# A filter's hand-over between two steps: 16 block transpositions in SBUF in place of a round trip through DRAM

## The chip, the cores, the metric

The kernel runs on one core of a Trainium2 chip. The metric is the device time of one execution, in microseconds (us), as the median of several runs. All timed runs quoted here are of the fast state (the state in which executions of one kernel agree within some tenths of a per cent: ten of the kernel before took 2589.09 to 2597.96 us). A time that comes from a profile is the span of the profiled execution, which is some 2 us shorter than the timed figure of that same execution.

## The reference

A spectral filter along the sequence, then an MLP mixer; eight batches of 3008 x 256 floats.

```python
X = np.fft.rfft(x, axis=1)                        # x: (8, 3008, 256)
y = np.fft.irfft(X * (filt_r + 1j * filt_i)[None], n=3008, axis=1)
h = np.maximum(y.transpose(0, 2, 1) @ w_tok1, 0.0) @ w_tok2     # token mixing
u = y + h.transpose(0, 2, 1)
out = u + np.maximum(u @ w_ch1, 0.0) @ w_ch2                    # channel mixing
```

## The kernel before

The length 3008 is split as 64 x 47. The filter's *first step* (`a_unit`) is a product over the 64, with 12 tiles per batch. Its result has on each partition one pair of a frequency k2 (32 of them) and one of four parts, and along the row 24 places times 256 columns. The *second step* (`b_unit`, then `bi_unit`) takes, for one k2 at a time, the four parts times 24 places as 96 rows. So rows must change partitions in between. The kernel did this through a DRAM buffer `z`:

```python
def a_unit(b, c):
    ps = bank(free_bank())
    nc.tensor.matmul(ps, wa, xs.pop((b, c)).rearrange("p a d -> p (a d)"), start=True, stop=True)
    t1 = t1p.tile([P, XC, D], FP32, tag="t1", name="t1")          # two buffers
    nc.scalar.copy(out=t1.rearrange("p a d -> p (a d)"), in_=ps)
    nc.scalar.dma_start(rows_of(z_d, b)[:, ts(c, XC), :], t1)     # 256 KB out
# ... (cut) in dft(), second step:
    def t2_load(c):
        where, tag = (sp, "s") if first and c % 3 == 2 else (t2p, "t2")
        t2s[c] = where.tile([KR, KC, nb, D], FP32, tag=tag, name="t2")
        for i, b in enumerate(bs):
            nc.sync.dma_start(t2s[c][:, :, i, :], z_d[b, ts(c, KC)].rearrange("k r d -> r k d"))  # 192 KB in
    def b_unit(k):
        # ... (cut)
        nc.tensor.matmul(ps, wbs[k // WC][0:KR, k % WC, 0:P], t2s[k // KC][:, k % KC], start=True, stop=True)
        # ... (cut) fr, fi: the filter
        nc.vector.tensor_tensor(out=p1, in0=ps, in1=fr, op=ALU.mult)
        nc.vector.scalar_tensor_tensor(out=p2[re], in0=ps[im], scalar=-1.0, in1=fi, op0=ALU.mult, op1=ALU.mult)
        nc.vector.tensor_tensor(out=p2[im], in0=ps[re], in1=fi, op=ALU.mult)
```

The filters of batches 1 to 7 run beside the mixer of earlier batches. The first batch's filter has nothing to hide behind: it runs alone, beside the rounding of the mixer's 64-bit weights, and the mixer starts after it.

## Time and profile before

| | kernel before |
|---|---|
| time, median of 4 runs (beside the changed kernel) | 2592.37 us (2590.78 to 2594.97) |
| span of the profile | 2590.2 us |
| last matmul of the first step begins | 35.38 us |
| first product of the second step begins ("the mark") | 48.57 us |
| second step (first product to end of last product) | 76.99 us, to 125.56 |
| first matmul of the mixer begins | 169.77 us |

One more view: the DMA queues of the first 36 us. The columns are packets, MB, and share of the time of the 16 DMA engines; q1 is SyncE's queue, q10 ScalarE's, q0 GpSimd's.

```profile
q1 hardware_dynamic: 2930, 5.56, 56.2%
q10 hardware_dynamic: 1930, 2.93, 23.3%
q0 software_dynamic: 640, 0.58, 7.0%
```

Nearly all of the 23.3% are the stores of z (11 of 256 KB in this stretch).

### The profile page before, as it was taken

To read this page: it belongs to the slowest core of one execution; us is meant where nothing else is said; L and a number is where in the kernel's file an instruction comes from. 1 tells how busy PE (TensorE), PEld (TensorE's weight loads), DVE (VectorE), ACT (ScalarE), POOL (GpSimd) and SP (SyncE) were. 2 spreads that over 40 slices of the span, in tenths; PEclk is the share of its full clock that TensorE was granted. 3 is DMA by queue.
4 is the path that set the end of the run, shared out by engine and by line. 5 is a ranking of instruction groups with operands and counts; after the bars stand their busy time and mean duration, and the time that the engine had idled before them with its cause. 6 is when DMAs were issued, how large, how long until landed. Compare 5 with 4: busy or idle time off the path is not lost.

```text
span 2590.2 us, 31521 instructions
## 1 busy us (share of the span) xinstructions
PE 2510.2 (97%) x10952; PEld 2002.7 (77%) x10952; DVE 1795.7 (69%) x3441; ACT 691.2 (27%) x1347; POOL 527.7 (20%) x966
## 2 busy tenths in 40 slices
PE   6889999999999999999999999999999999999998
PEld 2556766788888777888887777788888888888887
DVE  3796888556575888745666788846678576647676
ACT  2433222123321222212231222212222122212222
POOL 3553111111211112112112111121121121211212
PEclk7999999999999999999999999999999999999999
DMA  8974333312332322203232223211232121100001
GB/s 235 251 199 154 110 100 110 109 48 85 95 90 63 88 82 77 80 13 93 90 95 79 75 83 86 81 32 57 90 85 74 51 64 52 25 9 8 17 12 21
DMA packets 156746, 211.43 MB, mean 82 GB/s; under 512 B 34648, under 2 KB 105410, under 8 KB 156588
## 3 DMA queue, kind: packets, MB, share of 16 engines
q1 hardware_dynamic: 84396, 118.80, 16.0%
q0 software_dynamic: 30656, 39.93, 6.4%
q10 hardware_dynamic: 41536, 50.69, 6.1%
q8 instruction: 87, 1.43, 0.2%
q14 instruction: 71, 0.58, 0.1%
HBM read 134.31 MB, written 74.97 MB: 81 GB/s over the span
## 4 chain that ended last, share of the span: by engine, by line
PE 76%; DVE 12%; ACT 2%; issue 2%; DMA 1%; ACTq 0%; DVEq 0%; POOL 0%; SPq 0%; POOLq 0%
PE ps_po L612 27%; PE ps_pg L578 16%; PE ps_pg L594 11%; PE ps_b L538 4%; PE ps_b L521 3%; DVE t L556 3%; DVE hh L556 2%; PE ps_acc L521 2%; PE ps_acc L538 2%; PE ps_b L543 2%; PE ps_acc L407 2%; DVE u L556 2%; PE ps_acc L475 1%; PE ps_b L475 1%; DVE s L556 1%
## 5 line engine op out<-in xcount | busy, mean ns | idle before, releaser
L556 DVE TENSOR_TENSOR hh<-ps_pg,s 128x512 f32<-128x512 f32 (+3 forms) x864 | 481.9, 585 | 626.4 <-ACT s L581 625.9
L657 POOL DMA_DIRECT2D out_dram<-r x757 | 410.6, 551 | 1948.7 <-ACT hh L599 928.4
L599 ACT ACTIVATE hh<-hh 128x512 f32<-128x512 f32 (+1 forms) x576 | 347.8, 621 | 1119.7 <-DVE hh L556 1119.7
L612 PE MATMUL ps_po<-t,wc 128*128 128x256 f32 (+1 forms) x2304 | 535.3, 375 | 5.1 <-DVE t L556 4.4
L612 PEld LDWEIGHTS ps_po<-t,wc 128*128 128x128 f32 x2304 | 434.6, 190 | 132.3 <-issue 54.1
L612 PE MATMUL ps_po<-hh,wc 128*128 128x256 f32 (+1 forms) x1728 | 413.2, 375 | 3.1 <-POOL wc L329 2.8
L578 PE MATMUL ps_pg<-v,wc 128*128 128x256 f32 (+1 forms) x1728 | 413.7, 375 | 0.8 <-POOL wc L328 0.7
L612 PEld LDWEIGHTS ps_po<-hh,wc 128*128 128x128 f32 x1728 | 327.5, 190 | 42.4 <-POOL wc L329 3.6
L578 PEld LDWEIGHTS ps_pg<-v,wc 128*128 128x128 f32 x1728 | 327.3, 190 | 41.4 <-DVE v L556 3.0
L594 PE MATMUL ps_pg<-u,wc 128*128 128x256 f32 (+1 forms) x1152 | 293.6, 377 | 7.4 <-DVE hh L556 7.0
L556 DVE TENSOR_TENSOR t<-t,hh 128x256 f32<-128x256 f32 (+1 forms) x576 | 242.0, 420 | 19.8
L594 PEld LDWEIGHTS ps_pg<-u,wc 128*128 128x128 f32 x1152 | 215.6, 190 | 43.8 <-DVE hh L556 17.7
L556 DVE TENSOR_TENSOR s<-ps_pg,hh 128x512 f32<-128x512 f32 (+1 forms) x288 | 196.1, 681 | 30.7 <-DVE hh L556 0.9
L556 DVE TENSOR_TENSOR t<-hh 128x512 f32<-128x512 f32 (+1 forms) x288 | 192.2, 667 | 0.6 <-ACT hh L599 0.6
L578 PE MATMUL ps_pg<-u,wc 128*128 128x256 f32 (+1 forms) x576 | 170.4, 378 | 3.0 <-DVE hh L556 3.0
L594 PE MATMUL ps_pg<-v,wc 128*128 128x256 f32 (+1 forms) x576 | 168.8, 375 | 0.0
L581 ACT COPY s<-ps_pg 128x256 f32<-128x256 f32 (+1 forms) x288 | 106.0, 368 | 153.2 <-PE ps_pg L578 150.1
L578 PEld LDWEIGHTS ps_pg<-u,wc 128*128 128x128 f32 x576 | 102.8, 191 | 22.1 <-issue 8.2
L594 PEld LDWEIGHTS ps_pg<-v,wc 128*128 128x128 f32 x576 | 108.5, 190 | 13.2
L521 PE MATMUL ps_b<-t,w 128*128 128x256 f32 x480 | 106.3, 384 | 3.2 <-ACT both L235 2.4
L538 PE MATMUL ps_b<-w,h 128*128 128x512 f32 (+1 forms) x232 | 107.7, 587 | 0.0
L475 PE MATMUL ps_acc<-p,wb 128*96 128x256 f32 (+1 forms) x256 | 95.4, 474 | 11.9 <-ACT t L481 7.3
(92 smaller groups left out, 2236.1 us busy)
## 6 DMA issues: line engine op xcount, KB each, us to landing
z_tmp<-t ACTq DMA_DIRECT2D x96, 256.0 KB
t<-z_tmp SPq DMA_DIRECT2D x128, 192.0 KB
g_tmp<-t ACTq DMA_DIRECT2D x128, 192.0 KB
x<-in_x_dram SPq DMA_DIRECT2D x184, 128.0 KB
out_dram<-r POOLq DMA_DIRECT2D x698, 32.0 KB, 1.8
t<-g_tmp SPq DMA_DIRECT2D x42, 512.0 KB
wb<-wbi_t SPq DMA_DIRECT2D x80, 224.0 KB
filt<-in_filt_r_dram SPq DMA_DIRECT2D x128, 48.0 KB
```

What stands on the lines that cost most here:

```text
L407: nc.tensor.matmul(ps, wa, xs.pop((b, c)).rearrange("p a d -> p (a d)"), start=True, stop=True)
L475: nc.tensor.matmul(ps[0:KR], wbs[k // WC][:, k % WC, P:], p, start=(i == 0), stop=(i == len(parts) - 1))
L521: nc.tensor.matmul(acc[:, t, :], w1[:, a, ts(t, P)], t4[b, a // TC4][:, a % TC4, :], start=(a == 0 and t == 0), stop=(a == A - 1 and t == ...
L538: nc.tensor.matmul(ps[:, 0:w], h1[:, t, ts(dh, P)], w2[:, t, ds(m * 512, w)], start=(t == 0), stop=False)
L543: nc.tensor.matmul(ps[:, ds(q * P, n)], t4[b, c][:, r, ts(dh, P)], wai[:, 0:n], start=False, stop=(q == 3))
L556: nc.vector.tensor_tensor(out=out, in0=in0, in1=in1, op=op)
L578: nc.tensor.matmul(ps[:, 0:hw], wc1[:, jp, n, :], mov, start=True, stop=True)
L581: nc.scalar.copy(out=s[:, 0], in_=g[0][:, 0, 0:hw])
L594: nc.tensor.matmul(ps[:, 0:hw], wc1[:, jp, n, :], mov, start=True, stop=True)
L599: nc.scalar.activation(out=hs, in_=hs, func=AF.Relu)
L612: nc.tensor.matmul(po[i][:, j, 0:hw], wc2[:, jp, n, :], mov, start=(jp == 0 and first == 1), stop=(jp == JP - 1 and last == 1))
L657: q.dma_start(rows[g, e, :, ds(h * A + 4 * m, n)], blocks[ts(g, CW), h, e, 0:n])
```

## The change

For batch 0 alone, `z` is replaced by a tile `turned` that holds all 24 places (and 8 of zeros, to make 32) by 256 columns. The first step's table is reordered, so that one part's 32 frequencies lie on 32 neighbouring partitions. Then 16 in-place transpositions of 32x32 blocks exchange frequency and place inside each group of 32 partitions. The second step's matmuls read 128 rows (with zero weights for the padding) straight from `turned`. The mixer's channel weights later take the tile's memory.

```diff
+    wa0 = wa.reshape(P, K2, 4).transpose(0, 2, 1).reshape(P, P)
+    wbi0 = wbi.copy()
+    wbi0[:, :, 0:P] = 0
+    wbi0.reshape(4, K2, K2, P + KR)[:, 0:A, :, 0:P] = wb.reshape(4, A, K2, P)
 ... (cut)
+    turned = wcp.tile([P, K2 * D + P], FP32, tag="wc", name="turned")
+    wa0 = turned[:, K2 * D:]
+    turned = turned[:, 0:K2 * D].rearrange("p (s d) -> p s d", d=D)
 ... (cut) a_unit:
-        nc.tensor.matmul(ps, wa, xs.pop((b, c)).rearrange("p a d -> p (a d)"), start=True, stop=True)
+        nc.tensor.matmul(ps, wa0 if b == 0 else wa, xs.pop((b, c)).rearrange("p a d -> p (a d)"), start=True, stop=True)
+        if b == 0:
+            nc.scalar.copy(out=turned[:, ts(c, XC), :].rearrange("p a d -> p (a d)"), in_=ps)
+            return
 ... (cut) between the steps:
+        if first:
+            for d in range(0, D, 16):
+                v = turned.rearrange("p s d -> p d s")[:, d:d + 16, :]
+                nc.vector.transpose(v, v)
 ... (cut) b_unit:
-            nc.tensor.matmul(ps, wbs[k // WC][0:KR, k % WC, 0:P], t2s[k // KC][:, k % KC],
-                             start=True, stop=True)
+            t2 = turned[:, k, :].unsqueeze(1) if first else t2s[k // KC][:, k % KC]
+            nc.tensor.matmul(ps, wbs[k // WC][0:P if first else KR, k % WC, 0:P], t2, start=True, stop=True)
 ... (cut) at the start:
+        nc.vector.memset(turned[:, A:K2, :], 0.0)
```

More of the change, by code (lines that the diff above doesn't have):

```diff
@@ L115, in _make_tables @@
     wbi[:, :, P:] = wi
-    return wa.astype(f), wai.astype(f), wbi.astype(f)
+    wa0 = wa.reshape(P, K2, 4).transpose(0, 2, 1).reshape(P, P)
+    wbi0 = wbi.copy()
+    wbi0[:, :, 0:P] = 0
+    wbi0.reshape(4, K2, K2, P + KR)[:, 0:A, :, 0:P] = wb.reshape(4, A, K2, P)
+    return wa.astype(f), wa0.astype(f), wai.astype(f), wbi.astype(f), wbi0.astype(f)
 @with_exitstack
@@ L132 @@
     nc = tc.nc
-    wa_np, wai_np, wbi_np = _make_tables()
+    wa_np, wa0_np, wai_np, wbi_np, wbi0_np = _make_tables()
     wa_d = nc.inline_tensor(wa_np, name="wa_t").ap()
@@ L139 @@
     wbi_d = nc.inline_tensor(wbi_np, name="wbi_t").ap()
+    wa0_d = nc.inline_tensor(wa0_np, name="wa0_t").ap()
+    wbi0_d = nc.inline_tensor(wbi0_np, name="wbi0_t").ap()
     z_d = nc.dram_tensor("z_tmp", (B, K2, KR, D), FP32, kind="Internal").ap()
@@ L148 @@
     glob = pool("glob", 1)
+    wcp = pool("wcp", 1)
     xp = pool("xp", XB)
@@ L188 @@
     w2 = glob.tile([P, TC, A * P], FP32, name="w2")
-    wc1 = glob.tile([P, JP, 7, P], FP32, name="wc1")
-    wc2 = glob.tile([P, JP, 7, P], FP32, name="wc2")
+    turned = wcp.tile([P, K2 * D + P], FP32, tag="wc", name="turned")
+    wa0 = turned[:, K2 * D:]
+    turned = turned[:, 0:K2 * D].rearrange("p (s d) -> p s d", d=D)
+    chan = []
     def raw(src, row, ap):
@@ L338, in wc1_load @@
         yield from rounded(st, 512, [(lambda v: v.rearrange("p (i j n) -> p i j n", j=2, n=P),
-                           wc1[:, 2 * q:2 * q + 2, slice(0, 5, 4) if c == 0 else slice(1, 7, 5)])], late)
+                           chan[0][:, 2 * q:2 * q + 2, slice(0, 5, 4) if c == 0 else slice(1, 7, 5)])], late)
         if c == DH - 1:
             for jp in range(2 * q, 2 * q + 2):
-                combine(wc1[:, jp:jp + 1])
+                combine(chan[0][:, jp:jp + 1])
     def wc2_load(i):
@@ L351, in tile_of @@
             return lambda v: v.rearrange("p (j g e i) -> p e j g i", j=2, e=DH, i=CW)[:, dh]
-        yield from rounded(st, 512, [(tile_of(dh), wc2[:, i, n].rearrange("p j (g i) -> p j g i", i=CW))
+        yield from rounded(st, 512, [(tile_of(dh), chan[1][:, i, n].rearrange("p j (g i) -> p j g i", i=CW))
                           for dh, n in ((0, slice(0, 2)), (1, slice(4, 7, 2)))], True)
-        combine(wc2[:, i:i + 1])
+        combine(chan[1][:, i:i + 1])
     LAST = ((wc2_load, 0), (wc1_load, 1), (wc1_load, 4), (wc2_load, 1), (wc1_load, 2), (wc2_load, 2), (wc1_load, 5),
@@ L421, in w_load @@
                 wbs[g] = wbp.tile([P, WC, P + KR], FP32, tag="wb", name="wb")
-                nc.sync.dma_start(wbs[g], wbi_d[:, ts(g, WC), :])
+                nc.sync.dma_start(wbs[g], (wbi0_d if first else wbi_d)[:, ts(g, WC), :])
             filt_load(c, first)
@@ L437, in dft @@
         t2s, t3s, prods = {}, {}, {}
+        if first:
+            for d in range(0, D, 16):
+                v = turned.rearrange("p s d -> p d s")[:, d:d + 16, :]
+                nc.vector.transpose(v, v)
         def t2_load(c):
-            where, tag = (sp, "s") if first and c % 3 == 2 else (t2p, "t2")
-            t2s[c] = where.tile([KR, KC, nb, D], FP32, tag=tag, name="t2")
+            if first:
+                return
+            t2s[c] = t2p.tile([KR, KC, nb, D], FP32, tag="t2", name="t2")
             for i, b in enumerate(bs):
@@ L577, in up_first @@
                            (g[1][:, 0], 6, vt[:, 0, 0:hw]), (g[1][:, 1], 4, vt[:, 1, 0:hw])):
-            nc.tensor.matmul(ps[:, 0:hw], wc1[:, jp, n, :], mov, start=True, stop=True)
+            nc.tensor.matmul(ps[:, 0:hw], chan[0][:, jp, n, :], mov, start=True, stop=True)
         s = sp.tile([P, 3, 256], FP32, tag="s", name="s")[:, :, 0:hw]
@@ L593, in up_last @@
                            (g[1][:, 1], 3, vt[:, 3, 0:hw])):
-            nc.tensor.matmul(ps[:, 0:hw], wc1[:, jp, n, :], mov, start=True, stop=True)
+            nc.tensor.matmul(ps[:, 0:hw], chan[0][:, jp, n, :], mov, start=True, stop=True)
         h = hh[:, :, 0:hw]
@@ L611, in down @@
         for i, j, first, last, n, mov in todo[part]:
-            nc.tensor.matmul(po[i][:, j, 0:hw], wc2[:, jp, n, :], mov, start=(jp == 0 and first == 1),
+            nc.tensor.matmul(po[i][:, j, 0:hw], chan[1][:, jp, n, :], mov, start=(jp == 0 and first == 1),
                              stop=(jp == JP - 1 and last == 1))
@@ L748 @@
     with tc.manual_schedule():
-        nc.sync.dma_start(wa, wa_d)
+        nc.sync.dma_start(wa0, wa0_d)
+        nc.vector.memset(turned[:, A:K2, :], 0.0)
         for t in filts:
@@ L755 @@
             if i == 0:
-                for t, src in ((wai_t, wait_d), (wai, wai_d), (ident, ident_d)):
+                for t, src in ((wai_t, wait_d), (wa, wa_d), (wai, wai_d), (ident, ident_d)):
                     nc.scalar.dma_start(t, src)
@@ L782 @@
         sum_up()
+        both = wcp.tile([P, 2, JP, 7, P], FP32, tag="wc", name="wc")
+        chan.extend((both[:, 0], both[:, 1]))
         for i in range(rounds, A // 2 + TC * N2 // NG):
```

## The prediction

> **What bounds the kernel now.** I read the page first, then the busy time by stretch, then the engines' timelines of the first 130 us, then the waits. The page says that the span as a whole belongs to TensorE:
>
> ```profile
> PE 2510.2 (97%) x10952; PEld 2002.7 (77%) x10952; DVE 1795.7 (69%) x3441; ACT 691.2 (27%) x1347; POOL 527.7 (20%) x966
> ```
>
> The change touches the filter of the first batch only, so what counts is when that filter runs and what bounds the kernel there. The busy time by stretch (length, then each engine's busy us with its instruction count, the granted clock, the DMA share, GB/s) shows it; I chose the cuts from the timelines (last matmul of the first step near 36, first product of the second step at 48.57, last one at 127, first matmul of the mixer at 169.77):
>
> ```profile
> 0.00:36.00 36.00, 18.95 (x23) 5.86 (x24) 9.45 (x15) 9.49 (x15) 11.07 (x24) 0.78 0.87 252
> 36.00:48.57 12.57, 6.12 (x9) 2.48 (x8) 0.00 (x0) 2.35 (x4) 0.00 (x0) 0.64 0.86 235
> 48.57:127.00 78.43, 70.04 (x236) 41.25 (x236) 64.98 (x144) 33.43 (x69) 47.71 (x87) 0.94 0.94 243
> ...
> 215.00:2590.00 2375.00, 2343.30 (x10412) 1903.03 (x10412) 1642.02 (x3134) 614.26 (x1203) 416.06 (x769) 1.00 0.24 69
> ```
>
> From 215 us on TensorE is busy 2343.3 of 2375 us; nothing of the change lies there, except that it begins earlier or later. Before 36 us no engine is full, but the DMA engines are (0.87, 252 GB/s). Between 36 and 48.57 VectorE does nothing at all, which is the time in which z goes to DRAM and comes back. From 48.57 to 127 VectorE has 65.0 of 78.4 us, and DMA is at 0.94. The VectorE and TensorE timelines show the hand-over (start, length, engine, line, operation, and in brackets the idle time before it with what ended it):
>
> ```profile
> 35.38 2.05 PE L407 MATMUL ps_acc<-x,wa 128*128 128x512 f32 x2 [5.71 <-DMA x<-in_x_dram]
> ...
> 47.29 1.19 PE L450 MATMUL ps_b<-t,wb 96*128 96x256 f32 x2 [6.45 <-DMA t<-z_tmp]
> ...
> 48.57 0.42 DVE L463 TENSOR_TENSOR p<-ps_b,filt 128x256 f32<-128x256 f32 x1 [13.26 <-PE ps_b L450]
> ```
>
> The last matmul of the first step waits for its input x, whose loads share the DMA engines with the stores of z. After it come copy, store, load, and the first matmul of the second step at 47.29. So 48.57 us is the mark: from there VectorE runs nearly without a break, and a shift of that mark shifts the mixer, and the end, by as much.
>
> [...] the output's block transpositions of 512 elements take 701 ns, hardly more than the 681 to 693 ns of a two-input operation of that size. [...] The new transpositions step by one whole row of 256 floats, 1 KB, on the read side and on the write side[...]. The kernel before has one such write, the sums into w at L263, which step by 512 bytes:
>
> ```profile
> L644 DVE STREAM_TRANSPOSE r<-u 128x512 f32<-128x512 f32 x80 | 56.1, 701 | 0.0
> ...
> L263 DVE TENSOR_TENSOR w<-both 128x384 f32<-128x384 f32 x8 | 6.6, 830 | 0.3
> L263 DVE TENSOR_TENSOR w<-both 128x192 f32<-128x192 f32 x2 | 1.0, 487 | 0.1
> ```
>
> 830 less 487 over 192 elements is 1.79 ns per element. Dense, 681 less 426 ns over 256 elements gives 1.0. [...] the trace has no strided read. [...] x waits while z is stored from another engine's queue (DMA share 0.87).
>
> **The change, part by part.**
> Removed: 12 stores of z of 256 KB from ScalarE's queue, 16 loads of 192 KB from SyncE's, hence 3 MB out and 3 MB in, and the round trip ahead of 47.29. ScalarE also loses five waits, 8.6 us together, for the two buffers that the stores emptied.
>
> First step. Up to 36 us, the DMA queues' table of that stretch gives 56.2% of the engines' time to SyncE's queue (x, weights, tables), 23.3% to ScalarE's (nearly all z: 2.75 of 2.93 MB), 7.0% to GpSimd's; 86.5% together. Without z's 21.9 points, the same work takes 35.4 x (1 - 21.9/86.5) = 26.4 us. TensorE sets a floor: twelve pairs of matmuls of 1.9 to 2.05 us at its reduced clock (0.78 here), from 4.8 us on, are 28 us. I take the last pair to begin at 27.5 rather than 35.4; with 2.05 for the pair, 0.6 for the copy and the signals, the transpositions begin at 30.
>
> Added: 16 transpositions of 128x512 on VectorE, in place, all of which must end before the first matmul of the second step (each of them has only 16 of the 256 columns of a row). Dense they would be 16 x 0.70 = 11.2 us. With the strided slope, 0.17 fixed + 512 x 1.79 ns = 1.08 us each, 17.3 in all. That covers the write; the read is strided too. If reading and writing overlap fully it stays near 1.1; if they add up, 1.5. I choose 1.15 us, and 0.03 between two: 16 x 1.18 = 18.9 us. VectorE is idle at that time, but the path goes through it: 30 + 18.9 + 1.3 (from matmul to first product, as 47.29 to 48.57) = 50.2 us. That is 1.6 later than 48.57. Hence at this mark the gain of the shorter first step is about eaten by the transpositions.
>
> Also added: a memset of 8 x 256 zeros ahead of the filters' (two times 0.91 us, in idle time; the filter loads start 2 us later, with slack). The matmuls of the second step read 128 rows instead of 96: same columns, same duration.
>
> Second step, 48.57 to 127. VectorE's work is unchanged: 65.0 us busy, some 69 with the gaps of 0.03 us. The other 9 to 10 us are waits, most of them after 100 us, for filter loads and what hangs on them (3.7 us directly for the imaginary part, 2.2 for ScalarE's copy of the real part, which itself waits 10.5 us for its load; some more for TensorE behind that). A filter load takes 5.2 us to land (median), 2.0 at best. Of 12787 packets in the stretch, 13 loads of z of 192 KB in 1 KB rows are some 2500, a fifth. With a fifth less, DMA is no longer at its limit and I expect about half of these waits to go: -5 us. From 127 to 170 VectorE is full (37.2 of 42.8 us) and ScalarE waits 4.5 us for weights; -1 us from a quieter DMA.
>
> Moved: the mixer's weights take the place of the turned tile, which is free long before they are written (last use near 127, first write at 164): no cost. The sum is +1.6 - 5 - 1 = -4.4 us: 2593.4 - 4.4 = **2589 us**.
>
> **Rivals.** (1) *VectorE takes the place of the round trip*: if each strided transposition costs 1.5 us or more, the mark goes to 56 or beyond, and eats the rest: 2594; at 2.3 us (read and write each twice as slow and one after the other) the mark lies at 69, +20 - 6 = 2607. For it: both sides are strided, the read is unmeasured. [...] (2) *The transpositions run at the dense 0.70 us*: the mark at 42.8, with -6: 2582; if the second step also loses nearly all its waits, 2578. For it: the dense rows; against it: L263. (3) *The DMA relief is hidden*: the first step is held by TensorE's clock and by the order of loads (its x and weights still take 56.2% of DMA time), so that it ends at 33; the waits in the second step are GpSimd's issuing (47.7 us busy in 78, six filter loads of 0.55 us per pair of units), and stay. Then +6 - 1: 2599. (4) *The gain or loss does not reach the end*, because a later stage absorbs it: between 127 and 170 VectorE and TensorE are 87% and 93% busy, and beyond 215 TensorE 98.7%, so I see nothing to absorb more than 2 us.
>
> **Range and chances.** The duration of the transpositions weighs most: 0.70 to 1.5 us are 13 us of mark, the first step's end adds 4 either way, the second step's waits 4. That gives 2576 to 2602, 8 in 10. Two per cent are 52 us, four fifths of the first 65 us of the kernel: neither a gain nor a loss of that size fits in a part that ends at 48.57. Faster by over 2%: 0.01; within: 0.97; slower: 0.02.
>
> **What would show it right or wrong.** In the profile after: a group of 16 transpositions with its mean (right if 1.0 to 1.3 us); the last matmul of the first step beginning at 26 to 30 us; the first product of the second step near 50; the DMA share of the second step clearly under 0.94, the filter waits about halved, its length near 73 us instead of 78.4; the first matmul of the mixer near 165; from 215 us the same busy times as before. The prediction is wrong if the transpositions have another duration, if each waits for a signal, if the copies into one shared tile make matmuls and copies of the first step take turns, or if the second step keeps its length with less DMA, because GpSimd's issuing set it.

The costs come from the trace of the kernel before: 701 ns for a dense transposition of 512 elements, and 1.79 ns per element with a step of 512 bytes on the write side against 1.0 dense. That 1.15 us lies near full overlap of reading and writing (1.1) and not near their sum (1.5) was the estimate. That the second step's matmuls take as long on 128 rows as on 96 was measured only afterwards (379 against 381 ns).

## The result and the profile after

Ratios here are the mean time of one kernel's fast runs over that of the other's fast runs of the same rounds, so they are not quite the ratio of the medians beside them.

| | before | after |
|---|---|---|
| time, median of 4 runs | 2592.37 us | 2589.48 us (2588.01 to 2591.14) |
| ratio | | 0.9988, 95% interval 0.9971 to 1.0005 |
| last matmul of the first step | 35.38 | 28.44 |
| the mark | 48.57 | 49.52 |
| second step | 76.99 us | 72.61 us |
| end of the last product to the mixer's first matmul | 44.21 us | 45.25 us |
| the mixer's first matmul | 169.77 | 167.38 |
| from there to the end | 2420.4 us | 2419.8 us |

The time is the same within 2%. The outputs are right. The profile's 3.0 us are the sum of the table's lines: +0.95 at the mark, -4.38 in the second step, +1.04 up to the mixer, -0.6 after it.

The timelines of TensorE and VectorE after the change, the same hand-over as in the prediction (start, length, engine, line, operation; in brackets the idle time and what ended it):

```profile
28.44 2.04 PE L417 MATMUL ps_acc<-x,turned 128*128 128x512 f32 x2 [2.57 <-DMA x<-in_x_dram]
...
48.24 1.19 PE L470 MATMUL ps_b<-turned,wb 128*128 128x256 f32 x2 [15.34 <-issue]
...
31.14 17.00 DVE L455 STREAM_TRANSPOSE turned<-turned 128x512 f32<-128x512 f32 x16 [1.87 <-ACT turned L419]
49.52 0.42 DVE L482 TENSOR_TENSOR p<-ps_b,filt 128x256 f32<-128x256 f32 x1 [1.39 <-issue]
```

TensorE's 15.34 us of idle time bear the label "issue" because the profile shows no releaser, but the transpositions end at 48.14 and the matmul follows at 48.24. A group's row gives the mean of the new operation:

```profile
L455 DVE STREAM_TRANSPOSE turned<-turned 128x512 f32<-128x512 f32 x16 | 17.0, 1156 | 1.9 <-ACT turned L419 1.9
```

The mean is 1.16 us (median 1.152), yet 16 of them take 17.00 us, 1.06 us from one start to the next: each begins some 0.1 us before the one ahead is recorded as ended.

The DMA queues of the first 36 us, after:

```profile
q1 hardware_dynamic: 3587, 7.40, 82.6%
q0 software_dynamic: 640, 0.58, 6.9%
q10 hardware_dynamic: 576, 0.26, 3.0%
```

The stores are gone from q10, but q1 has filled the room: 7.40 MB instead of 5.56, since 16 loads of weights of 256 KB were issued in this time instead of 11. The DMA engines are busier than before (a share of 0.93 of the 36 us against 0.87), though they move less (229 against 252 GB/s).

The busy time by stretch, cut at each kernel's own mark, end of last product, and 215 us (columns as in the prediction); first before, then after:

```profile
48.57:125.56 76.99, 68.60 (x231) 40.15 (x230) 63.68 (x140) 33.10 (x68) 47.71 (x87) 0.94 0.94 245
125.56:169.77 44.21, 41.08 (x157) 28.96 (x158) 38.46 (x80) 16.61 (x29) 14.81 (x27) 0.96 0.77 193
```

```profile
49.52:122.13 72.61, 66.29 (x231) 38.26 (x230) 63.56 (x140) 33.04 (x68) 48.14 (x87) 0.98 0.82 212
122.13:167.38 45.25, 41.09 (x156) 28.97 (x157) 38.48 (x81) 16.58 (x29) 15.36 (x29) 0.96 0.75 195
...
215.00:2587.20 2372.20, 2340.42 (x10407) 1901.05 (x10406) 1641.23 (x3132) 613.39 (x1201) 414.40 (x767) 1.00 0.24 69
```

VectorE does the same work in the second step (63.6 us, 140 instructions) in 4.4 us less, at a DMA share of 0.82 instead of 0.94. The 64 matmuls on 128 rows take 379 ns (median), as those on 96 rows did (381).

What VectorE waited for on account of the filter, between 48 and 126 us (us in total, times, longest); first before, then after:

```profile
DVE p L464 <- DMA filt<-in_filt_i_dram: 3.7, 2, 2.1
DVE p L463 <- ACT filt L215: 2.2, 3, 0.8
```

```profile
DVE p L482 <- ACT filt L225: 2.0, 2, 1.7
DVE p L483 <- DMA filt<-in_filt_i_dram: 1.5, 3, 0.7
```

These waits fell from 5.9 to 3.5 us. With the others that the same view lists after the mark (4.0 before, 2.2 after: for products of TensorE, or without a label) that makes 9.9 against 5.7 us, about the step's gain.

What became of the gain after the second step is on TensorE's timeline; the first line is of the kernel before, the second of the kernel after:

```profile
139.31 22.64 PE L521 MATMUL ps_b<-t,w 128*128 128x256 f32 x96 [2.37 <-ACT both L235]
```

```profile
136.93 22.64 PE L540 MATMUL ps_b<-t,w 128*128 128x256 f32 x96 [3.40 <-DMA t<-g_tmp]
```

The token sums now wait for the other round trip, the filter's result that goes through DRAM (`g_tmp`), where before a conversion of weights was last. This is one profile: in the third one below, TensorE did not wait there at all, but 2.76 us later on, for VectorE's sums of weights (`w`), and the mixer started no earlier (169.56).

### The profile page after: what moved, and what is told of

Same layout as the page of the kernel before. It is cut to its first block, busy times and chain, and to the rows that moved or that the text cites. A ratio compares the mean times of both kernels' runs of the same rounds, so it can differ in the third digit from the quotient of the medians.

```text
span 2587.2 us, 31459 instructions
## 1 busy us (share of the span) xinstructions
PE 2505.6 (97%) x10952; PEld 2000.9 (77%) x10952; DVE 1816.0 (70%) x3458; ACT 691.2 (27%) x1347; POOL 526.9 (20%) x966
## 4 chain that ended last, share of the span: by engine, by line
PE 78%; DVE 13%; issue 3%; DMA 3%; ACT 2%; SPq 0%; ACTq 0%; POOL 0%; DVEq 0%; POOLq 0%
PE ps_po L631 26%; PE ps_pg L597 15%; PE ps_pg L613 11%; PE ps_b L540 4%; PE ps_b L557 4%; DVE t L575 3%; DVE hh L575 3%; PE ps_acc L540 2%; PE ps_acc L557 2%; PE ps_acc L494 2%; PE ps_b L562 2%; PE ps_acc L417 2%; DVE u L575 2%; DVE s L575 1%; PE ps_b L470 1%
## 5 line engine op out<-in xcount | busy, mean ns | idle before, releaser
L540 PEld LDWEIGHTS ps_b<-t,w 128*128 128x128 f32 x480 | 92.2, 192 | 17.9 <-issue 4.0
```

The costliest lines, as they stand in the source:

```text
L540: nc.tensor.matmul(acc[:, t, :], w1[:, a, ts(t, P)], t4[b, a // TC4][:, a % TC4, :], start=(a == 0 and t == 0), stop=(a == A - 1 and t == ...
```

## The experiments

Each profile was read at the same points: last matmul of the first step, the mark, the second step's length, the mixer's first matmul. The theory at the outset: the kernel's end follows the mark one for one; the strided transpositions decide where the mark lies; the second step got shorter because z's loads are gone.

**How well a single profile repeats.** The changed kernel itself was run twice more.

> The changed kernel once more, as the reference for the other runs of this call. Ratio to the kernel before 0.9988 as first measured (0.9980 to 0.9996); first product of the second step at 49.5 us, second step 72.6 us long, mixer's first matmul at 167.4.

> The changed kernel again, as the reference for the run with pairs in the same call: ratio to the kernel before 0.998, mixer's first matmul between 163 and 168.

| changed kernel | mark | second step | mixer's first matmul | span | ratio (95%) |
|---|---|---|---|---|---|
| first | 49.52 | 72.61 | 167.38 | 2587.2 | 0.9988 (0.9971 to 1.0005) |
| again | 48.70 | 71.50 | 163.14 | 2583.2 | 0.9981 (0.9968 to 0.9993) |
| third | 49.91 | 73.92 | 169.56 | 2589.2 | 0.9992 (0.9979 to 1.0006) |

The third start of the mixer, 169.56, lies outside the expected 163 to 168, and the second, 163.14, is 4 us ahead of what was expected. The mark repeats within 1.2 us and the second step's length within 2.4, but the stretch from there to the mixer took 45.3, 42.9 and 45.7 us. So a single profile carries some 6 us of scatter in the mixer's start. Of the kernel before there is one profile only. I compare below with the changed kernel: "again" for the runs with loads, with stores and with 128-byte steps, "third" for the runs with pairs and with stores from a constant. The others are compared with the first changed run. They were run at other times.

**Dense transpositions** (wrong result).

```diff
-                v = turned.rearrange("p s d -> p d s")[:, d:d + 16, :]
+                v = turned.rearrange("p s d -> p (s d)")[:, 32 * d:32 * d + 512].rearrange("p (d s) -> p d s", s=K2)
```

> The changed kernel with the same 16 transpositions in place, but each on 512 neighbouring floats instead of floats 1 KB apart. Wrong result on purpose; nothing else differs. Theory (the stride sets their duration, and the mark of the second step, and with it the end, follows one for one): 0.70 us each as in the output's block transpositions instead of 1.15, some 10 us in all instead of 17.0; first product of the second step at 42.3 instead of 49.5; mixer's first matmul near 160.1 instead of 167.4; end 7 us earlier, near 2582 us. Rival A (a fixed cost or the in-place operation sets the duration, not the stride): still 1.15 us each, nothing moves. Rival B (a later stage absorbs it, as loads of weights and filters are not ready earlier): first product at 42.3, but mixer's first matmul after 164 and the end less than 4 us earlier.

VectorE's timeline of this run:

```profile
29.73 9.61 DVE L455 STREAM_TRANSPOSE turned<-turned 128x512 f32<-128x512 f32 x16
39.26 0.39 DVE L482 TENSOR_TENSOR p<-ps_b,filt 128x256 f32<-128x256 f32 x1
```

A transposition took 671 ns, where those with the 1 KB step took 1152; all of them took 9.61 us (0.60 from one start to the next). Rival A (a fixed cost) falls: the stride sets the duration. The mark came at 39.26, earlier than the expected 42.3, because this edit also loosened a dependency: the first matmul reads a block that one of the first transpositions finishes, so it no longer waits for all 16. The transpositions also begin before ScalarE's last copy (29.73; that copy starts at 31.1). The median was 2578.94 us, ratio 0.9941 (0.9925 to 0.9958). The mark lies 10.3 us ahead of the first changed run; the mixer's first matmul (156.89) and the span (2577.2) lie 10.5 and 10.0 us ahead. Rival B (absorbed later) is not seen.

**One side strided** (wrong result): eight transpositions read with the 1 KB step and write dense, eight the other way round.

```diff
+                w = turned.rearrange("p s d -> p (s d)")[:, 32 * d:32 * d + 512].rearrange("p (d s) -> p d s", s=K2)
-                nc.vector.transpose(v, v)
+                nc.vector.transpose(*((w, v) if d < D // 2 else (v, w)))
```

> The changed kernel with one side of each transposition made dense: the first 8 read 1 KB apart and write neighbouring floats, the last 8 the other way round. Wrong result on purpose. Theory (the sides overlap, so that one strided side alone sets the pace): both halves at 1.15 us like the original. Rival C (each side adds its own part): both halves near 0.92 us. Rival D (only one side pays): one half at 0.70, the other at 1.15 us.

The groups of this run, in a window around the first eight and one around the last eight:

```profile
L456 DVE STREAM_TRANSPOSE turned<-turned 128x512 f32<-128x512 f32 x8 | 8.3, 1043 | 0.8 <-ACT turned L419 0.6
```

```profile
L456 DVE STREAM_TRANSPOSE turned<-turned 128x512 f32<-128x512 f32 x8 | 8.3, 1038 | 0.3
```

Each side alone costs about the same, 1.04 us, and both together 1.15. That lies between the theory's 1.15 and the 0.92 of a sum of two parts, nearer to the theory, and neither side is free. The first strided side adds 0.37 us to the dense 0.67, the second only 0.11: reading and writing overlap for the most part. All 16 took 17.17 us here and 17.00 with both sides strided, but these paces can't be compared: here each transposition touches floats that another one writes, and each begins 0.03 us after the one ahead has ended (1.075 us from start to start), where in the changed kernel it begins 0.1 us earlier than that end.

**No transposition at all** (wrong result; the loop is deleted).

> The changed kernel without any transposition. Wrong result on purpose. Theory (one for one): first product of the second step near 33 instead of 49.5, mixer's first matmul near 151, end 16 us earlier, near 2573 us. Rival B (the filter and weight loads of the first 130 us, which had 17 us of quiet DMA to catch up, become the bound): the second step takes longer than 72.6 us by 5 us or more, and the end is less than 11 us earlier.

VectorE's timeline at the mark:

```profile
37.05 0.42 DVE L477 TENSOR_TENSOR p<-ps_b,filt 128x256 f32<-128x256 f32 x1 [6.53 <-ACT filt L225]
```

The mark came at 37.05, not at 33: without the transpositions, the next to end is ScalarE's copy of the filter, which stands in ScalarE's order behind a weight conversion. So the transpositions cost 12.5 us of the mark, not their full 17. The second step took 71.86 us, so rival B (loads that can't keep up) is refuted. The mixer's first matmul (151.86) and the span (2571.4) came 15.5 and 15.8 us earlier than in the first changed run, 3 us more than the mark, which is within the scatter above. The median was 2574.98, ratio 0.9928 (0.9913 to 0.9943).

**The transpositions three times** (result right, since an even number of extra ones cancels).

```diff
-            for d in range(0, D, 16):
+            for d in 3 * list(range(0, D, 16)):
```

> The changed kernel with the 16 transpositions done three times, result right. Theory (one for one): 48 transpositions take 51 us, first product near 83.5, mixer's first matmul near 201.4, end 34 us later, near 2623 us. Rival B (slack further on takes part of it): end less than 28 us later.

```profile
31.15 50.59 DVE L455 STREAM_TRANSPOSE turned<-turned 128x512 f32<-128x512 f32 x48 [0.95 <-ACT turned L419]
83.13 0.42 DVE L482 TENSOR_TENSOR p<-ps_b,filt 128x256 f32<-128x256 f32 x1 [1.39 <-issue]
```

The mark is 33.6 us later than in the first changed run, the mixer's first matmul (201.14) 33.8 later, the span (2621.8) 34.6 later; median 2621.73, ratio 1.0107 (1.0092 to 1.0122). In this direction too, the end follows the mark one for one.

**The second step's loads put back.** The 16 loads of 192 KB return to SyncE's queue; they read the input and nobody uses them.

```diff
             if first:
+                dummy = t2p.tile([KR, KC, 1, D], FP32, tag="t2", name="t2")
+                nc.sync.dma_start(dummy[:, :, 0, :], x[0][ds(c * 187, KC * KR)].rearrange("(k r) d -> r k d", k=KC))
                 return
```

> The changed kernel, with the 16 loads of the second step put back on SyncE's queue: as many bytes in as many rows of 1 KB, read from the input and never used; result right. Theory (the second step became 4.4 us shorter because these loads no longer crowd the filter and weight loads): DMA share of the step back near 0.94 from 0.82, its length back from 72.6 to 76 to 78 us, mixer's first matmul near 171. Rival (the step is shorter for another reason, as what its matmuls wait for, or the weights converted during the transpositions): length 72 to 74 us.

The second step's row of the busy time by stretch, in this run:

```profile
50.62:128.06 77.44, 66.63 (x231) 38.03 (x230) 63.58 (x140) 33.00 (x68) 48.23 (x87) 0.98 0.93 231
```

The step is back at 77.44 us and 0.93 of DMA time: the whole gain of the second step is gone, with VectorE's and GpSimd's work unchanged. VectorE's filter waits are back too, at 8.5 us (5.9 before, 3.5 after the change). TensorE's granted clock, the row's third figure from the end, is not what made the step shorter: it rose from 0.94 to 0.98 with the change, and is 0.98 here too. The loads of the filter's imaginary part (48 KB) took 5.2 us to land in the kernel before, 4.0 after the change, and 6.0 here. The median rose to 2597.61, ratio 1.0020 (1.0004 to 1.0036). That is more than the step's 5.9 us over the changed kernel "again": the mark was 1.9 us later and the stretch before the mixer 1.3 us longer.

**The first step's stores put back, from the turned tile.**

```diff
             nc.scalar.copy(out=turned[:, ts(c, XC), :].rearrange("p a d -> p (a d)"), in_=ps)
+            nc.scalar.dma_start(rows_of(z_d, b)[:, ts(c, XC), :], turned[:, ts(c, XC), :])
             return
```

> The changed kernel, with the 12 stores of z in the first step put back on ScalarE's queue, straight from the turned tile, with no two small buffers between and nobody who reads them; result right. Theory (the first step ended 7 us earlier because x no longer shares the DMA engines with the stores): last matmul of the first step back from 28.4 to near 35, first product near 56. Rival (it ended earlier because ScalarE no longer waits for its two store buffers, 8.6 us in the kernel before): last matmul stays near 29 to 30.

The last matmul came at 34.14, as expected, but the mark at 62.60 instead of 56, with this on VectorE's timeline:

```profile
44.27 16.94 DVE L456 STREAM_TRANSPOSE turned<-turned 128x512 f32<-128x512 f32 x16 [8.92 <-DMA st<-in_moe_w_tok_dram]
```

In place, the transpositions must also wait until the stores have read the tile, and I had overlooked this. (The profile names the transfer that landed last before; that it was the stores is read from the program, not shown by this line. The record of the DMA packets agrees: ScalarE's queue, which has only these stores then, still moves packets until 43.4 us, and none from 43.6 to 44.27.) So this run says nothing about the mark.

**The stores put back, from a constant.** As before, but the stores read a block of zeros beside the tile, so that nothing waits for them.

```diff
+            nc.scalar.dma_start(rows_of(z_d, b)[:, ts(c, XC), :], zeros.rearrange("p (a d) -> p a d", d=D))
```

> As the run with the stores put back, but the 12 stores read a constant block of zeros, so that nothing waits for them (the earlier one made the transpositions wait until its stores had read the tile); result right. Theory (the first step ended earlier because the stores no longer share the DMA engines with x): last matmul of the first step near 34 again (28.4 to 29.7 without stores, 35.4 before), first product near 55, end 6 us later than the changed kernel's. Rival (the stores shift nothing by themselves; the earlier run's delay came from ScalarE's waits): last matmul at 29 to 30, first product near 50.

TensorE's and VectorE's timelines:

```profile
33.72 1.27 PE L418 MATMUL ps_acc<-x,turned 128*128 128x512 f32 x2 [2.96 <-DMA x<-in_x_dram]
```

```profile
35.65 16.99 DVE L457 STREAM_TRANSPOSE turned<-turned 128x512 f32<-128x512 f32 x16 [0.34 <-ACT turned L420]
54.03 0.42 DVE L484 TENSOR_TENSOR p<-ps_b,filt 128x256 f32<-128x256 f32 x1 [1.39 <-issue]
```

The last matmul begins at 33.72 instead of 29.26 ("third"), the mark is at 54.03 instead of 49.91. So sharing the DMA engines with the stores accounts for 4.5 of the 6.1 to 6.9 us by which the changed kernel's first step ends earlier than at 35.38. (The run before, at 34.14, has 5.6 over "again".) The other 2 us I can't assign with certainty; the two store buffers of the kernel before are a candidate that no run isolates.

**A dense layout with steps of 128 bytes.** The tile is laid out as columns by places, so that the transpositions are dense; in exchange ScalarE writes, and TensorE reads its moving operand, 128 bytes apart. Result right.

```diff
-    turned = turned[:, 0:K2 * D].rearrange("p (s d) -> p s d", d=D)
+    turned = turned[:, 0:K2 * D].rearrange("p (d s) -> p d s", s=K2)
-            nc.scalar.copy(out=turned[:, ts(c, XC), :].rearrange("p a d -> p (a d)"), in_=ps)
+            nc.scalar.copy(out=turned[:, :, ts(c, XC)].rearrange("p d a -> p a d"), in_=ps.rearrange("p (a d) -> p a d", d=D))
-                v = turned.rearrange("p s d -> p d s")[:, d:d + 16, :]
+                v = turned[:, d:d + 16, :]
-            t2 = turned[:, k, :].unsqueeze(1) if first else t2s[k // KC][:, k % KC]
+            t2 = turned[:, :, k].unsqueeze(1) if first else t2s[k // KC][:, k % KC]
```

> A correct version that should beat both: the turned tile is laid out with the 32 places of a column side by side, so the 16 transpositions are dense. ScalarE's copies write 128 bytes apart and TensorE reads its moving operand 128 bytes apart. Theory: transpositions 0.70 us each, 10 us in all; ScalarE's copies 1.0 us instead of 0.59, with slack but for the last; first product near 43; if TensorE reads at full pace, second step as long as in the changed kernel, end 6 to 7 us earlier than the changed kernel's. Rival (TensorE's strided reads cost): the second step's first matmuls take clearly over 0.38 us, 64 of them at twice the time are 24 us of TensorE's time, and part or all of the gain is lost.

The tile's view (duration in ns as minimum, median, maximum; then first and last start):

```profile
L470 PE MATMUL ps_b<-turned,wb x32: 590/607/766, 42.0 to 113.4; 128*128 128x256 f32 x32
...
L455 DVE STREAM_TRANSPOSE turned<-turned x16: 670/674/714, 32.2 to 41.2; 128x512 f32<-128x512 f32 x16
```

The transpositions are fast and the mark comes at 43.24, but the rival holds as well: the matmuls take 607 ns instead of 379, ScalarE's copies 1.03 us instead of 0.59, and the second step 75.67 us instead of 71.50. The ratio, 0.9970 (0.9955 to 0.9985), can't be told from the changed kernel's 0.9981. The stride's cost had only been moved.

**Pairs.** So far a step of 1 KB (VectorE, 1.15 us) and steps of 128 bytes (ScalarE 1.03 us, TensorE 607 ns) were slow, and dense access (0.67 us, 0.59 us, 379 ns) was not; nothing between had been tried. That two neighbouring floats at each step might be enough was the guess. So two neighbouring places of a column are put side by side, and pairs of places 2 KB apart. The transpositions then touch two neighbouring floats before each step of 2 KB; ScalarE and TensorE step by 8 bytes. Result right.

```diff
-    turned = turned[:, 0:K2 * D].rearrange("p (s d) -> p s d", d=D)
+    turned = turned[:, 0:K2 * D].rearrange("p (h d r) -> p h d r", d=D, r=2)
-            nc.scalar.copy(out=turned[:, ts(c, XC), :].rearrange("p a d -> p (a d)"), in_=ps)
+            nc.scalar.copy(out=turned[:, c].rearrange("p d r -> p r d"), in_=ps.rearrange("p (r d) -> p r d", d=D))
-                v = turned.rearrange("p s d -> p d s")[:, d:d + 16, :]
+                v = turned.rearrange("p h d r -> p d h r")[:, d:d + 16]
-            t2 = turned[:, k, :].unsqueeze(1) if first else t2s[k // KC][:, k % KC]
+            t2 = turned[:, k // 2, :, k % 2].unsqueeze(1) if first else t2s[k // KC][:, k % KC]
-        nc.vector.memset(turned[:, A:K2, :], 0.0)
+        nc.vector.memset(turned[:, A // 2:], 0.0)
```

> A correct version that should beat both: the turned tile keeps two neighbouring places of a column side by side (8 bytes), pairs 2 KB apart, [...] and TensorE's moving operand and ScalarE's copies step by 8 bytes only. Theory[...]: transpositions 0.67 to 0.70 us, some 10 us in all; TensorE's first matmuls of the second step stay at 0.38 us; copies at 0.59; first product at 42 to 43; second step 71 to 73 us; mixer's first matmul 7 us earlier than in the changed kernel of the same call; ratio to the kernel before 0.995. Rival A[...]: transpositions 1.04 us and more, nothing gained. Rival B (TensorE slows at any step but one): its matmuls 0.6 us as in the layout with 128-byte steps, second step 75 us.

The tile's view and VectorE's timeline:

```profile
L470 PE MATMUL ps_b<-turned,wb x32: 385/388/767, 40.6 to 107.9; 128*128 128x256 f32 x32
...
L455 DVE STREAM_TRANSPOSE turned<-turned x16: 671/671/714, 30.9 to 39.8; 128x512 f32<-128x512 f32 x16
```

```profile
30.89 9.61 DVE L455 STREAM_TRANSPOSE turned<-turned 128x512 f32<-128x512 f32 x16 [0.90 <-ACT turned L419]
41.89 0.42 DVE L482 TENSOR_TENSOR p<-ps_b,filt 128x256 f32<-128x256 f32 x1 [1.39 <-issue]
```

Pairs are enough: the transpositions take 671 ns, just as the dense ones did, the matmuls 388 ns (9 more than at step one), the copies 0.61 us. (Only VectorE touches adjacent floats here, 671 ns; ScalarE, 0.61 us, and TensorE, 388 ns, touch every second float. Why these steps cost next to nothing and the long ones do, no run shows, nor from which step on.) The mark is 8.0 us and the mixer's first matmul (159.34) 10.2 us earlier than in the changed kernel; 2.3 of the 10.2 are a shorter second step (71.58 against 73.92 us), which is within the scatter. Median 2583.09 against 2591.05 for that kernel; ratio to the kernel before 0.9965 (0.9953 to 0.9978), where the changed kernel had 0.9992 (0.9979 to 1.0006). This version beats both kernels, if by a third of a per cent, which still counts as the same at 2%: its six runs (2581.86 to 2584.43) lie below every run of either (lowest 2585.29).

## Why the prediction was right

It said 2589 us, 2576 to 2602, and "within 2%" with 0.97; measured were 2589.48 us. This is not luck of one run (the two further medians are 2587.92 and 2591.05). That the total fits to half a microsecond is luck, though: the forecast change was -4.4 us and the measured one -2.9, from a base of 2593.4 (three runs) that a fourth run lowered to 2592.37, and some terms of the sum missed in opposite directions.

- **Where it matters.** Right. All differences lie before the mixer, and the end follows the mark one for one (dense, three times). That nothing further on absorbs a shift was rival 4, and three experiments with marks from 37 to 83 us deny it (in the one without transpositions, within 3 us).
- **The first step.** Predicted: last pair from 35.4 to 27.5; measured 28.4 to 29.3. The mechanism, x sharing the DMA engines with the stores, was shown with stores from a constant (33.7). The sum by shares of DMA time (26.4) was too kind because it kept the other traffic fixed: the freed time was taken up by weights, and x is still what the last matmul waits for (2.57 us). The floor of 28 us from TensorE's clock was misread: pairs of matmuls took down to 1.10 us in the profile before, and down to 1.02 after, so nothing held the twelve to 1.9 us each. That 27.5 came close is therefore luck in part.
- **The transpositions.** Predicted 1.15 us each, with a choice between full overlap and sum of the two strided sides; measured 1.152. That reading and writing mostly overlap is shown by the run with one strided side (1.04, where the slope from L263 gave 1.08); the match to the last digit is luck, as 1.15 was picked between 1.1 and 1.5. The term that was mis-sized is the gap: 0.03 us between two was assumed, while they overlap by 0.1; so 17.0 us instead of 18.9. That offset the later start (31.1 instead of 30).
- **The mark.** Predicted 50.2, measured 48.7 to 49.9. The gain of the first step is eaten by the transpositions, as foreseen.
- **The second step.** Predicted -5 us by relieved filter loads, with the filter waits about halved; measured -3.1 to -5.5 in three profiles against the one of the kernel before, DMA share 0.82, filter waits 3.5 us instead of 5.9 (2.7 in each of the two further profiles). The forecast's 78.4 us for the step before ran to 127; to the end of its last product it took 76.99. Putting the loads back restored 77.4 us. That refutes rival 3's part about GpSimd's issuing, whose busy time was the same in these runs (47.7 us before, 48.1 after, 48.2 with the loads put back).
- **Between the second step and the mixer.** Predicted -1 us; measured -1.3 to +1.5, in the first profile +1.04. This term failed: other waits (the filter's result through DRAM, the weights) take the place of those that went, and the stretch scatters by nearly 3 us from run to run.
- **Rival 1** (1.5 us or more for each transposition) did not come true, as they took 1.15; VectorE did take the place of the round trip, but at the size in the forecast itself. **Rival 3**'s other part, a first step held to 33 us, is refuted by 28.4. **Rival 2**, dense speed, was wrong for the kernel as it was, but the pairs made it true, with 2583.1 us where it said 2582.
- **Two slips.** The 12787 packets belong to the stretch from 48 to 128 us; from 48.57 to 127 they are 12604, and z's loads a fifth of either. In rival 3, a first step to 33 moves the mark by 7 us by the prediction's own sum, not 6.

What stays open: the 2 us of the first step not explained by the stores, and what sets the scatter before the mixer.

## What to carry to other kernels

The round trip through DRAM had two prices in this kernel: its latency at the hand-over (13.2 us from the last matmul of the first step to the mark) and the DMA time that it took from everything else (the second step took 77.0 us with z's loads, 72.6 without, 77.4 with as many loads put back). Here a trade of the latency for as long a chain on VectorE left only the second, some 4 us. Before a strided operation is accepted, ask whether its layout can keep the elements in neighbouring pairs, and measure it: here a layout of pairs served three engines at once, where a layout dense for one engine only moved the cost to another. The sizes measured on 4-byte floats:

| | long step | pairs | dense |
|---|---|---|---|
| VectorE, block transposition of 128x512 (step of 1 KB; in pairs 2 KB) | 1.04 us with one strided side, 1.15 us with both | 671 ns | 671 ns |
| ScalarE, copy of 128x512 (step of 128 bytes; in pairs 8 bytes) | 1.03 us | 0.61 us | 0.59 us |
| TensorE, matmul with a moving operand of 256 columns (step of 128 bytes; in pairs 8 bytes) | 607 ns | 388 ns | 379 ns |

The in-place transpositions also waited for stores that still read the tile, which is an order that the program sets: with stores from the turned tile the transpositions began at 44.3 us, with a constant as the source at 35.7.
